# Values laid out and summed like keys on 128 partitions, their sums transposed on TensorE, and the first pass planned anew

## The chip, the cores and the metric

The kernel runs on one core of a Trainium2 chip. The metric is the device time of one execution in microseconds (us): the median of several executions. All times before come from three executions and from one more that was profiled.

## What is computed

Attention over pooled keys and values, and behind it two gated layers, all in 32-bit floats:

```python
B, H, S, D = 8, 8, 576, 64              # q, k, v
k_p = k.reshape(B, H, 72, 8, D).mean(axis=3)
v_p = v.reshape(B, H, 72, 8, D).mean(axis=3)
scores = D ** -0.5 * q @ k_p.T           # per head: 576 x 72
attn = softmax(scores)
x = (attn @ v_p) as 4608 tokens x 512
h = x @ w_in;  g = h * sigmoid(1.702 * h);  x = g @ w_out          # d_ff 2048
out = ((x @ w_a) * (x @ w_b)) @ w_o2                                # d_ff 1536
```

## The kernel before

The 4608 tokens are 9 blocks of 512 (called j), a block is 4 units of 128 tokens (called u, 36 of them), and a batch has 576 tokens, so 4.5 units. The layers run in passes over all blocks. The first pass also holds the whole attention, and makes the first 2 to 6 of the 16 feed-forward chunks (called f) of each block. The later passes are not touched.

The work of the first pass is a list of small tasks that `first_tasks` writes with what each waits for and which buffers it takes and gives back. The names are: `lk`, `lv` load half of a batch's keys or values (4 heads of 8); `skr`, `sv` sum 8 neighbours on VectorE (DVE); `ska` copies key sums into the block-diagonal tile `kbd` on ScalarE (ACT); `lq` loads a unit's queries; `sc` are the scores on TensorE (PE); `mx` the maxima (DVE), `ex` the exponentials (ACT), `b2` the division (DVE); `pt` the transposes of the attention weights (PE, tile `pt`) and `cp` their copy (ACT, tile `aT`); `px` the product with the value sums (PE); `hi` and `lo` split its result into two parts of a block's `x` (ACT, DVE); `xh`, `xl` store that; `lw` loads half of a weight chunk and `cva`, `cvb`, `cvh`, `cvl` turn it from 64-bit words into a two-part tile `w` (ACT, DVE); `h` are the 12 matmuls of the first product of a chunk, `th`, `st`, `gh`, `gl` its gate; `y` the second product into four `acc` tiles; `ev` and `ys` evict and store them through two `ys` buffers. A block's first `h` needs all four `lo` of its block.

`first_plan` places the tasks on the engines by the table COST and some lengths beside it (DELAY), with priorities shifted by LEAN, and the program then issues them in that order; every engine keeps it (`pin`). Where PE would idle before the first `y`, it gets matmuls on a tile `busy` whose result nobody reads. The DMAs all go through one queue, that of SP, in plan order; the built program lets a DMA there wait for the eighth one before it, among others. In the built program a `sc`, `px` or `busy` matmul of the listing is two in the trace, a transpose is one.

Before, the values of a batch lie with the 72 pooled positions on the partitions: a load is 72 rows, of 2048 numbers for batches 0 and 1 (half a batch, 576 KB) and of 1024 for the others (a quarter, 288 KB), and the sum is a reduction on 72 partitions, L474. The keys lie with two heads' 64 columns on 128 partitions: 128 rows of 1152 numbers, 576 KB, L447, summed at L453.

Of the kernel before, what the change touches and what calls it, by code (L numbers as in the profile page):

```python
# [10 lines left out]
F32 = mybir.dt.float32  # L11
# [3 lines left out]
ALU = mybir.AluOpType  # L15
AX = mybir.AxisListType
# [8 lines left out]
UNIT = 128  # L25

COST = dict(
    k=1.51, q=.67, v=1.51, vq=.76, w=1.34, x=2.69, p=.67,
    skr=1.28, ska=.68, sc=.49, mx=.40, ex=1.19, b2=1.12, pt=.44, cp=.50, px=.48, hi=.51, lo=.61, sv=2.21, svq=1.14,
    cva=.58, cvb=1.53, cvh=.54, cvl=2.40, h=2.72, th=.51, st=.61, gh=.54, gl=.61, y=.682, eva=.51, evd=.61,  # L30
)
DELAY = dict(PE=.24, ACT=.12, DVE=.12, SP=2.2)
TURN = .1
ROOM = dict(ps=4, acc=3, at=2, aT=3, tmp=2, g=1, gg=2, ks=2, kraw=1, vraw=2, q=2, xs=3, raw=2, yp=2, w=19)
LEAN = dict(
    svq=-12, cvl=-6, skr=-14, v=-5, k=3, mx=29, cp=37, vq=8, cvb=-4, cvh=-20, h=-1, q=3, pt=26, gl=13, sv=4,
    ex=6, th=41, gh=-4, w=-10, ska=7, cva=6, sc=1, eva=-1,
)
SPARE_UNITS = 6
LOOSE_UNITS = 14  # L40
FILL = 2.5
ACT_EVICTS = 3

# [1 line left out]
def first_tasks(counts, seq, chunks_made, per):  # L45
# [11 lines left out]
    for b in range(nb * per * UNIT // seq):  # L57
        scored, used = [], []
        if b >= 2:
            last = ((b - 1) * seq - 1) // UNIT  # L60
            scored = [f"sc{last}.{e}" for e in range(2)]
            used = [f"px{last}.{e}" for e in range(2)]
        for e in range(2):
            home = ["w"] if b < 2 else ["kraw"]
            add(f"lk{b}.{e}", "SP", "k", takes=home)
            add(f"skr{b}.{e}", "DVE", "skr", [f"lk{b}.{e}"], ["ks"], home)
            add(f"ska{b}.{e}", "ACT", "ska", [f"skr{b}.{e}"] + scored, (), ["ks"])
        for e in range(2 if b < 2 else 4):
            home = ["w"] if b < 2 else ["vraw"]
            add(f"lv{b}.{e}", "SP", "v" if b < 2 else "vq", takes=home)  # L70
            add(f"sv{b}.{e}", "DVE", "sv" if b < 2 else "svq", [f"lv{b}.{e}"] + used, (), home)
    for u in range(nb * per):
        j = u // per
        bank = "any" if u < SPARE_UNITS else "ps"
# [11 lines left out]
        for e in range(2):  # L86
            back = ([f"px{u - 1}.0"] if e else [f"px{u - 2}.1"]) if u >= per else [f"px{u - 2}.{e}"] if u >= 2 else []
            add(
                f"pt{u}.{e}", "PE", "pt", [f"b2{u}"] + back + ([f"pt{u}.0"] if e else []), [bank],
                ([] if u == 2 else ["w"] if u == 3 else ["at"]) if e else [],  # L90
            )
            add(f"cp{u}.{e}", "ACT", "cp", [f"pt{u}.{e}"], ["aT"], [bank])
            need = [n for b in batches(u) for n in ([f"sv{b}.{e}"] if b < 2 else [f"sv{b}.{2 * e}", f"sv{b}.{2 * e + 1}"])]
# [55 lines left out]
def first_plan(tasks):  # L149
# [41 lines left out]
    while len(start) < len(tasks):  # L191
# [16 lines left out]
        for p in members.get(n, [n]):  # L208
            kind = tasks[p][1]
            for r in tasks[p][3]:  # L210
                if r == "any":
                    r = bank[holder(p)] = "acc" if room["acc"] > 0 else "ps"
                room[r] -= 1
            start[p] = s
            s += COST[kind]
            if engine == "PE":
                s += 0. if (kind in ("h", "y")) == large else TURN
                large = kind in ("h", "y")
            free[engine] = s
            end = s + DELAY[engine]  # L220
            for r in tasks[p][4]:
                heapq.heappush(gives, (end, bank[holder(p)] if r == "any" else r))
            for m in after[p]:
                left[m] -= 1
                ready[m] = max(ready.get(m, 0.), s if tasks[m][0] == engine else end)
                if not left[m]:
                    queue[tasks[m][0]].append(m)
    return start, bank
# [3 lines left out]
def tile_kernel(ctx, tc, q, k, v, w_in, w_out, w_a, w_b, w_o2, out):  # L232
# [13 lines left out]
    nc = tc.nc  # L246
    P = 128
    NU, _, NP, _ = q.shape
    B, SP, H, D, _ = v.shape
    NT, DM = out.shape  # L250
    S = SP * POOL
    DFF, DFF2 = w_out.shape[0], w_o2.shape[0]
# [161 lines left out]
        nc.gpsimd.memset(t, 0.0)  # L414

    q_t, ks_t, vs_t, at_t, aT_t, kraw_t, vraw_t = {}, {}, {}, {}, {}, {}, {}
    sc_t, pt_t, px_t, x_full = {}, {}, {}, {}

    def pieces(u):
# [6 lines left out]
            done += n  # L426

    scale = 1.0 / (POOL * D ** 0.5)
    V = 2
    early = {}  # L430

    def load_q(u):
# [8 lines left out]
    def load_k(b, half):  # L441

        if b < 2:
            raw = wp.tile([P, 2, S], F32, tag="w", name="kvraw")
        else:
            raw = ap_.tile([P, 2, S], F32, tag="kraw", name="kraw", bufs=1)
        pin("SP", nc.sync.dma_start(out=raw, in_=k[b, :, 2 * half:2 * half + 2, :]))  # L447
        kraw_t[b, half] = raw

    def sum_k(b, half):  # L450
        ks = ks_t[b, half] = ap_.tile([P, 2, SP], F32, tag="ks", name="ks", bufs=2)
        raw = kraw_t.pop((b, half)).rearrange("p c (s r) -> p c s r", r=POOL)
# [8 lines left out]
    def load_v(b, n):  # L461
        heads = H // 2 if b < 2 else V
        if b < 2:
            raw = wp.tile([SP, heads, D, POOL], F32, tag="w", name="kvraw")
        else:
            raw = ap_.tile([SP, heads, D, POOL], F32, tag="vraw", name="vraw", bufs=2)
        pin("SP", nc.sync.dma_start(out=raw, in_=v[b, :, n * heads:(n + 1) * heads]))
        vraw_t[b, n] = raw

    def sum_v(b, n):  # L470
        if b not in vs_t:
            vs_t[b] = ap_.tile([SP, H, D], F32, tag="vs", name="vs", bufs=2)
        heads = H // 2 if b < 2 else V
        pin("DVE", nc.vector.tensor_reduce(  # L474
            out=vs_t[b][:, n * heads:(n + 1) * heads, :], in_=vraw_t.pop((b, n)), op=ALU.add, axis=AX.X
        ))
# [755 lines left out]
```

## Time and profile before

| | us |
|---|---|
| three executions | 1782.6, 1787.7, 1789.05 |
| median | 1787.7 |
| the profiled execution, its own time | 1786.03 |
| its span, from the first to the last instruction | 1784.2 |
| PE busy / DVE busy / ACT busy in the span | 1749.2 / 1033.8 / 610.6 |

The span is the part that the trace shows; 1.8 us of the execution's time lie around it. A busy PE is one that has a matmul in its pipeline; the records overlap, and at a lower granted clock a matmul counts for longer, so busy time is not useful time.

### The profile page before, as it was taken

How to read it: one execution, taken by the hardware profiler on the slowest of the kernel's cores; microseconds unless marked ns; L12 is line 12 of the kernel's file. 1: busy time of each engine (PE TensorE's matmuls, PEld its weight loads, DVE VectorE, ACT ScalarE, POOL GpSimd, SP SyncE). 2: the span in 40 equal slices, each digit the busy share in tenths (PEclk: the TensorE clock that was granted, in tenths of full speed). 3: DMA queues.
4: the chain of work that ended last, by engine and by line, in shares of the span. 5: the costliest groups of instructions: out<-in, count | busy, mean ns of one | idle time of the engine just before them, and what ended most of it. 6: DMA issues, size and time to landing. Idle time of an engine off the chain costs nothing.

```text
span 1784.2 us, 22457 instructions
## 1 busy us (share of the span) xinstructions
PE 1749.2 (98%) x8610; PEld 1449.4 (81%) x8610; DVE 1033.8 (58%) x1769; ACT 610.6 (34%) x1495; POOL 1.7 (0%) x8
## 2 busy tenths in 40 slices
PE   7989999999999999999999999999999999999999
PEld 6778788888888888888887788878788888788887
DVE  6888996448526668677756655733444444434443
ACT  5767675433223323334333322222121211221121
POOL 0000000000000000000000000000000000000000
PEclk8999999999999999999999999999999999999999
DMA  7656652434312565636596785678545659536612
GB/s 241 212 195 227 211 181 93 177 118 130 112 53 118 183 216 224 230 155 254 204 361 248 289 303 178 227 272 333 203 136 182 242 208 333 227 129 238 236 56 89
DMA packets 86987, 357.99 MB, mean 201 GB/s; under 512 B 9728, under 2 KB 9728, under 8 KB 61888
## 3 DMA queue, kind: packets, MB, share of 16 engines
q1 hardware_dynamic: 86880, 356.55, 55.2%
q8 instruction: 68, 1.11, 0.3%
q14 instruction: 39, 0.32, 0.1%
HBM read 238.55 MB, written 117.96 MB: 200 GB/s over the span
## 4 chain that ended last, share of the span: by engine, by line
PE 87%; DVE 6%; DMA 5%; ACT 1%; issue 0%; SPq 0%; DVEq 0%; ACTq 0%
PE X L737 16%; PE Y L737 8%; PE acc L332 7%; PE acc L333 7%; PE acc L334 7%; PE h L332 7%; PE h L334 6%; PE h L333 6%; PE acc L692 5%; PE acc L690 5%; PE acc L691 5%; PE Z L737 4%; DMA part<-ys 2%; PE px L543 1%; PE pt L528 1%; PE sc L496 1%
## 5 line engine op out<-in xcount | busy, mean ns | idle before, releaser
L737 PE MATMUL X<-xo,wc 128*128 128x512 f32 (+1 forms) x1440 | 330.4, 370 | 5.2 <-DVE s L755 4.4
L737 PEld LDWEIGHTS X<-xo,wc 128*128 128x128 f32 x1440 | 255.5, 189 | 58.8 <-DVE s L755 11.7
L332 PE MATMUL h<-x,w 128*128 128x512 f32 x576 | 226.3, 393 | 1.3 <-DVE x L558 0.7
L333 PE MATMUL acc<-glo,w 128*128 128x512 f32 x576 | 225.5, 391 | 0.0
L334 PE MATMUL acc<-ghi,w 128*128 128x512 f32 x576 | 225.2, 391 | 0.0
L333 PE MATMUL h<-x,w 128*128 128x512 f32 x576 | 224.3, 389 | 0.4 <-DVE x L558 0.4
L334 PE MATMUL h<-x,w 128*128 128x512 f32 x576 | 224.3, 389 | 0.0
L332 PE MATMUL acc<-ghi,w 128*128 128x512 f32 x576 | 190.6, 397 | 3.2 <-ACT ys L1132 3.2
L737 PE MATMUL Y<-xo,wc 128*128 128x512 f32 (+1 forms) x720 | 167.5, 368 | 0.0
L660 DVE SCALAR_TENSOR_TENSOR g<-g,h 128x512 f32<-128x512 f32 x100 | 68.6, 686 | 154.3 <-ACT g L657 154.2
L722 ACT CAST ghi<-s 128x512 fp32r<-128x512 f32 (+1 forms) x60 | 34.7, 578 | 335.5 <-DVE s L756 335.5
L737 PEld LDWEIGHTS Y<-xo,wc 128*128 128x128 f32 x720 | 128.4, 189 | 23.7
L657 ACT ACTIVATE g<-h 128x512 f32<-128x512 f32 x100 | 59.8, 598 | 228.2 <-PE h L334 194.9
L751 DVE TENSOR_TENSOR s<-s,Y 128x512 f32<-128x512 f32 (+1 forms) x60 | 38.1, 634 | 170.5 <-PE Y L737 170.2
L332 PEld LDWEIGHTS acc<-ghi,w 128*128 128x128 f32 x576 | 108.6, 189 | 28.0 <-ACT ys L1132 3.7
L332 PEld LDWEIGHTS h<-x,w 128*128 128x128 f32 x576 | 108.1, 188 | 25.6 <-ACT aT L534 1.6
L334 PEld LDWEIGHTS acc<-ghi,w 128*128 128x128 f32 x576 | 108.8, 189 | 23.1
L333 PEld LDWEIGHTS h<-x,w 128*128 128x128 f32 x576 | 108.2, 188 | 22.5 <-DVE x L558 0.7
L334 PEld LDWEIGHTS h<-x,w 128*128 128x128 f32 x576 | 108.1, 188 | 22.6
L333 PEld LDWEIGHTS acc<-glo,w 128*128 128x128 f32 x576 | 108.7, 189 | 21.4
L798 DVE TENSOR_TENSOR part<-acc,part 128x512 f32<-128x512 f32 x72 | 49.7, 692 | 78.8 <-PE acc L692 78.5
L661 ACT CAST ghi<-g 128x512 fp32r<-128x512 f32 x100 | 62.2, 622 | 92.7 <-DVE g L660 64.2
(102 smaller groups left out, 2651.1 us busy)
## 6 DMA issues: line engine op xcount, KB each, us to landing
xo<-yd SPq DMA_DIRECT2D x84, 1024.0 KB
yd<-st SPq DMA_DIRECT2D x28, 1024.0 KB
part<-part SPq DMA_DIRECT2D x108, 256.0 KB
xd<-x SPq DMA_DIRECT2D x18, 1024.0 KB
part<-ys SPq DMA_DIRECT2D x72, 256.0 KB
x<-xd SPq DMA_DIRECT2D x18, 1024.0 KB
raw<-in_moe_w_out_dram SPq DMA_DIRECT2D x28, 512.0 KB
wd<-ws SPq DMA_DIRECT2D x12, 1024.0 KB
```

The source lines that it names most:

```text
L332: nc.tensor.matmul(out=o, lhsT=whi, rhs=xhi, start=first, stop=False),
L333: nc.tensor.matmul(out=o, lhsT=whi, rhs=xlo, start=False, stop=False),
L334: nc.tensor.matmul(out=o, lhsT=wlo, rhs=xhi, start=False, stop=last),
L657: nc.scalar.activation(out=g, in_=hps, func=AF.Tanh, scale=0.5 * 1.702)
L660: made = (nc.vector.scalar_tensor_tensor(out=g, in0=g, scalar=1.0, in1=hps, op0=ALU.add, op1=ALU.mult))
L661: nc.scalar.copy(out=ghi, in_=g)
L690: after_last(nc.tensor.matmul(out=oa, lhsT=chi[:, ts], rhs=whi, start=first, stop=False))
L691: after_last(nc.tensor.matmul(out=oa, lhsT=chi[:, ts], rhs=wlo, start=False, stop=False))
L692: after_last(nc.tensor.matmul(out=oa, lhsT=clo[:, ts], rhs=whi, start=False, stop=last))
L737: after_last(nc.tensor.matmul(out=banks[nm], lhsT=w[:, at_, we, ks], rhs=x[:, xe, kk, :], start=n in FIRST and kk == 0 and m == 0, stop=kk ...
L751: nc.vector.tensor_tensor(out=s[2], in0=s[2], in1=Y, op=ALU.add)
L798: nc.vector.tensor_tensor(out=t, in0=a, in1=t, op=ALU.add)
```

## The change

Three things change together.

- The values get the keys' layout, 128 partitions and 1152 numbers a load for every batch, and the same functions load (`load_kv`) and sum them (`sum_kv`). The sums then stand the wrong way round for `px`, so four transposes a batch on PE (`vt`) turn them into one PSUM bank, and one ACT copy (`vc`) puts that into the tile `vs`, which `px` reads as before.
- From batch 2 on, keys and values share one ring of two raw tiles instead of one for the keys and two for quarter values; the sums share a ring of four.
- The table of the planner is new: other lengths for loads and stores (weights 1.65 for 1.34, `x` 3.2 for 2.69), an extra lateness for stores, other room, and other priorities. So the whole order of the first pass is another one. What each block computes, and how many chunks it takes in the first pass, stays.

```diff
 COST = dict(
-    k=1.51, q=.67, v=1.51, vq=.76, w=1.34, x=2.69, p=.67,
-    skr=1.28, ... px=.48, hi=.51, lo=.61, sv=2.21, svq=1.14,
+    k=1.45, q=.67, v=1.45, w=1.65, x=3.2, p=.67,
+    skr=1.28, ... px=.48, hi=.51, lo=.61, sv=1.28, vt=.44, vc=.50,
 )
-DELAY = dict(PE=.24, ACT=.12, DVE=.12, SP=2.2)
+DELAY = dict(PE=.24, ACT=.12, DVE=.12, SP=2.3)
+LATE = dict(x=4., p=1.)
-ROOM = dict(..., aT=3, ..., ks=2, kraw=1, vraw=2, ...)
+ROOM = dict(..., aT=4, ..., ks=4, raws=2, vs=2, ...)
-LOOSE_UNITS = 14
+LOOSE_UNITS = 16
...
+        home, bank = (["w"], "any") if b < 2 else (["raws"], "ps")
         for e in range(2):
+            for load, total in (("lk", "skr"), ("lv", "sv")):
+                add(f"{load}{b}.{e}", "SP", load[1], takes=home)
+                add(f"{total}{b}.{e}", "DVE", total, [f"{load}{b}.{e}"], ["ks"], home)
             add(f"ska{b}.{e}", "ACT", "ska", [f"skr{b}.{e}"] + scored, (), ["ks"])
-        for e in range(2 if b < 2 else 4):
-            home = ["w"] if b < 2 else ["vraw"]
-            add(f"lv{b}.{e}", "SP", "v" if b < 2 else "vq", takes=home)
-            add(f"sv{b}.{e}", "DVE", "sv" if b < 2 else "svq", [f"lv{b}.{e}"] + used, (), home)
+        add(f"vt{b}", "PE", "vt", [f"sv{b}.{e}" for e in range(2)], [bank], ["ks", "ks"])
+        add(f"vc{b}", "ACT", "vc", [f"vt{b}"] + used, (), [bank])
...
-            need = [... f"sv{b}.{e}" ...]
+            need = [f"vc{b}" for b in batches(u)]
...
-                ready[m] = max(ready.get(m, 0.), s if tasks[m][0] == engine else end)
+                ready[m] = max(ready.get(m, 0.), s if tasks[m][0] == engine else end + LATE.get(tasks[m][1], 0.))
...
+    def turn_v(b):
+        vt = vt_t[b] = bank_of(f"vt{b}", [SP, NP, P])
+        for c in range(NP):
+            after_last(nc.tensor.transpose(vt[:, c, :], vsum_t[b, c // 2][:, c % 2, :], ident))
+
+    def copy_v(b):
+        vs_t[b] = ap_.tile([SP, H, D], F32, tag="vs", name="vs", bufs=2)
+        pin("ACT", nc.scalar.copy(out=vs_t[b].rearrange("s h d -> s (h d)"), in_=vt_t.pop(b).rearrange("s c n -> s (c n)")))
...
-        if name == "v":
-            return a.reshape(b, h, s // POOL, POOL, d).transpose(0, 2, 1, 4, 3)
         a = a.reshape(b, h // 2, 2, s, d).transpose(2, 4, 1, 0, 3)
-        if name == "k":
+        if name != "q":
             return a.transpose(3, 0, 1, 2, 4).reshape(b, 2 * d, h // 2, s)
```

The order moves everywhere in the first pass; two places are shown. First SP's queue near the start of the program, from the fourth query load on, before (`kvraw` and `vraw` are raw keys or values, `qs` and `q` queries, `raw` a weight half):

```order
L439 DMA qs<-in_q_dram 128x512
L439 DMA q<-in_q_dram 128x512 x2
L447 DMA kraw<-in_k_dram 128x1152
L467 DMA kvraw<-in_v_dram 72x2048
L467 DMA vraw<-in_v_dram 72x1024 x2
L467 DMA kvraw<-in_v_dram 72x2048 x2
L439 DMA q<-in_q_dram 128x512
L447 DMA kraw<-in_k_dram 128x1152
L439 DMA q<-in_q_dram 128x512
L467 DMA kvraw<-in_v_dram 72x2048
L640 DMA raw<-in_moe_w_in_dram 128x1024
L640 DMA raw<-in_moe_w_out_dram 128x1024
```

and the same place with the change, again from the fourth query load on:

```order
L441 DMA qs<-in_q_dram 128x512
L449 DMA kvraw<-in_v_dram 128x1152 x2
L449 DMA kvraw<-in_k_dram 128x1152
L634 DMA raw<-in_moe_w_in_dram 128x1024
L441 DMA q<-in_q_dram 128x512
L634 DMA raw<-in_moe_w_out_dram 128x1024
L441 DMA q<-in_q_dram 128x512
L449 DMA kvraw<-in_v_dram 128x1152 x2
L634 DMA raw<-in_moe_w_in_dram 128x1024
L449 DMA kvraw<-in_k_dram 128x1152 x2
L634 DMA raw<-in_moe_w_out_dram 128x1024
L441 DMA q<-in_q_dram 128x512 x2
```

The first weight halves moved from behind all values of batches 0 and 1, and behind values and keys of batch 2, to right behind batch 0's values; the values of batch 2 are no longer among the first loads.

Second, PE's order from the first product with values on (`px`; the scores of units 0 to 5 stand ahead of it). Before:

```order
L543 MATMUL px<-aT,vs 64x128 x8
L368 MATMUL busy<-ident 128x128 x6
L543 MATMUL px<-aT,vs 64x128 x8
L368 MATMUL busy<-ident 128x128 x11
L528 MATMUL pt<-ident,at_203 72x128 x16
L543 MATMUL px<-aT,vs 64x128 x8
L528 MATMUL pt<-ident,at 72x128 x4
L543 MATMUL px<-aT,vs 64x128 x4
L528 MATMUL pt<-ident,at 72x128 x4
L543 MATMUL px<-aT,vs 64x128 x4
L528 MATMUL pt<-ident,at 72x128 x4
L496 MATMUL sc<-kbd_136,q 128x144 x4
```

Behind these stand `px` and `pt` of units 4 and 5, more scores and two `busy`, and then the first `h`. With the change, from the last transposes ahead of the first `vt` on (scores of units 0 to 3 stand ahead):

```order
L522 MATMUL pt<-ident,at 72x128 x16
L370 MATMUL busy<-ident 128x128 x7
L466 MATMUL vt<-ident,ks 72x128 x4
L370 MATMUL busy<-ident 128x128 x3
L537 MATMUL px<-aT,vs 64x128 x4
L522 MATMUL pt<-ident,at_184 72x128 x4
L537 MATMUL px<-aT,vs 64x128 x4
L522 MATMUL pt<-ident,at_184 72x128 x4
L537 MATMUL px<-aT,vs 64x128 x4
L522 MATMUL pt<-ident,at_184 72x128 x4
L537 MATMUL px<-aT,vs 64x128 x4
L522 MATMUL pt<-ident,at_184 72x128 x4
```

Behind these stand 16 `px`, the scores of unit 4 (16 matmuls in the trace) and of half of unit 5's count (8), the second `vt`, three `busy`, and the first `h`. So before, six units are through their `px` ahead of the first `h`; with the change four are, and the scores of two more.

## Rows read from the trace of the kernel before

**Rows 1.** Busy time by stretch (--windows): PE, PEld, DVE, ACT, POOL, granted clock, DMA share, GB/s.
```profile
0.00:54.84 54.84, 41.93 (x310) 35.60 (x311) 34.39 (x56) 32.90 (x145) 1.73 (x8) 0.81 0.69 220
54.84:210.00 155.16, 146.83 (x951) 119.12 (x950) 139.29 (x249) 112.66 (x413) 0.00 (x0) 0.98 0.67 227
210.00:380.00 170.00, 169.19 (x1027) 140.80 (x1026) 109.88 (x200) 92.97 (x308) 0.00 (x0) 1.00 0.41 144
```

**Rows 2.** What PE waited for from 0 to 500: us in total, times, longest.
```profile
PE px L543 <- DVE vs L474: 5.9, 3, 4.0
PE pt L528 <- DVE at L522: 4.6, 2, 4.2
PE acc L332 <- ACT ys L1132: 3.2, 1, 3.2
```

**Rows 3.** PE's timeline, the first matmul of a feed-forward chunk: start, length.
```profile
54.84 0.47 PE L332 MATMUL h<-x,w 128*128 128x512 f32 x1
```

**Rows 4.** DVE's timeline, sums that waited for a load.
```profile
4.68 2.76 DVE L453 TENSOR_REDUCE ks<-kvraw 128x144 f32<-128x1152 f32 x2 [4.68 <-DMA kvraw<-in_k_dram]
...
8.98 1.35 DVE L453 TENSOR_REDUCE ks<-kvraw 128x144 f32<-128x1152 f32 x1 [0.28 <-DMA kvraw<-in_k_dram]
...
34.45 2.28 DVE L474 TENSOR_REDUCE vs<-kvraw 72x256 f32<-72x2048 f32 x1 [4.05 <-DMA kvraw<-in_v_dram]
```

**Rows 5.** PE's groups before 55 us (--lines): busy, mean ns; idle before.
```profile
L528 PE MATMUL pt<-ident,at 128*72 128x128 f32 x48 | 9.6, 361 | 5.2 <-DVE at L522 4.2 <-DVE sm L520 0.9
L543 PE MATMUL px<-aT,vs 72*64 72x128 f32 x80 | 8.4, 369 | 4.5 <-DVE vs L474 4.5
L496 PE MATMUL sc<-kbd,qs 128*128 128x144 f32 x32 | 5.0, 300 | 0.9 <-DMA qs<-in_q_dram 0.9
L496 PE MATMUL sc<-kbd,q 128*128 128x144 f32 x24 | 4.5, 344 | 0.0
```

**Rows 6.** The chain that ended last, in order of time: start, length, what.
```profile
43.43 1.00 PE pt L528 x4
44.43 1.05 PE px L543 x8
...
48.53 1.83 PE sc L496 x8
55.65 2.43 ACT at L512 x16
...
69.85 0.70 DVE raw L628
...
132.65 0.49 PE sc L496 x4
133.14 0.87 PE pt L528 x8
...
137.25 1.02 PE px L543 x16
```

**Rows 7.** Busy time by stretch again, two stretches of the start.
```profile
20.00:30.00 10.00, 5.49 (x48) 4.83 (x49) 5.60 (x6) 6.44 (x40) 0.00 (x0) 0.81 1.04 275
...
40.00:50.00 10.00, 10.00 (x59) 7.52 (x58) 4.24 (x11) 5.04 (x9) 0.00 (x0) 0.50 0.12 48
```

**Rows 8.** ACT's timeline: the first exponentials.
```profile
8.15 0.32 ACT L512 ACTIVATE at<-sc,mx 128x72 f32<-128x72 f32 x1
```

**Rows 9.** Groups of DVE and ACT from 0 to 380.
```profile
L474 DVE TENSOR_REDUCE vs<-vraw 72x128 f32<-72x1024 f32 x24 | 28.7, 1207 | 1.7 <-DMA vraw<-in_v_dram 1.7
...
L453 DVE TENSOR_REDUCE ks<-kraw 128x144 f32<-128x1152 f32 x12 | 16.1, 1346 | 2.4 <-DMA kraw<-in_k_dram 2.4
...
L534 ACT COPY aT<-pt 72x512 f32<-72x512 f32 x72 | 39.3, 589 | 20.9 <-PE pt L528 19.5 <-PE px L543 1.3
```

**Rows 10.** PE's transposes from 55 to 210 (--lines).
```profile
L528 PE MATMUL pt<-ident,at 128*72 128x128 f32 x136 | 18.5, 274 | 1.1 <-ACT aT L534 0.4 <-DVE at L522 0.4 <-ACT at L512 0.3
```

More of the change, by code (lines that the diff above doesn't have):

```diff
@@ L27 @@
 COST = dict(
-    k=1.51, q=.67, v=1.51, vq=.76, w=1.34, x=2.69, p=.67,
-    skr=1.28, ska=.68, sc=.49, mx=.40, ex=1.19, b2=1.12, pt=.44, cp=.50, px=.48, hi=.51, lo=.61, sv=2.21, svq=1.14,
+    k=1.45, q=.67, v=1.45, w=1.65, x=3.2, p=.67,
+    skr=1.28, ska=.68, sc=.49, mx=.40, ex=1.19, b2=1.12, pt=.44, cp=.50, px=.48, hi=.51, lo=.61, sv=1.28, vt=.44, vc=.50,
     cva=.58, cvb=1.53, cvh=.54, cvl=2.40, h=2.72, th=.51, st=.61, gh=.54, gl=.61, y=.682, eva=.51, evd=.61,
 )
-DELAY = dict(PE=.24, ACT=.12, DVE=.12, SP=2.2)
+DELAY = dict(PE=.24, ACT=.12, DVE=.12, SP=2.3)
+LATE = dict(x=4., p=1.)
 TURN = .1
-ROOM = dict(ps=4, acc=3, at=2, aT=3, tmp=2, g=1, gg=2, ks=2, kraw=1, vraw=2, q=2, xs=3, raw=2, yp=2, w=19)
+ROOM = dict(ps=4, acc=3, at=2, aT=4, tmp=2, g=1, gg=2, ks=4, raws=2, vs=2, q=2, xs=3, raw=2, yp=2, w=19)
 LEAN = dict(
-    svq=-12, cvl=-6, skr=-14, v=-5, k=3, mx=29, cp=37, vq=8, cvb=-4, cvh=-20, h=-1, q=3, pt=26, gl=13, sv=4,
-    ex=6, th=41, gh=-4, w=-10, ska=7, cva=6, sc=1, eva=-1,
+    mx=83, gl=42, lo=90, st=59, b2=57, px=21, pt=77, sv=2, vt=-3, gh=-19, ska=-29, cvh=-7, th=14, vc=5,
+    eva=-5, cp=-1, p=-8, evd=4, x=5,
 )
 SPARE_UNITS = 6
-LOOSE_UNITS = 14
+LOOSE_UNITS = 16
 FILL = 2.5
@@ L92, in first_tasks @@
             add(f"cp{u}.{e}", "ACT", "cp", [f"pt{u}.{e}"], ["aT"], [bank])
-            need = [n for b in batches(u) for n in ([f"sv{b}.{e}"] if b < 2 else [f"sv{b}.{2 * e}", f"sv{b}.{2 * e + 1}"])]
+            need = [f"vc{b}" for b in batches(u)]
             add(f"px{u}.{e}", "PE", "px", [f"cp{u}.{e}"] + need + ([f"px{u}.0"] if e else []), [] if e else [bank], ["aT"])
@@ L135, in holder @@
         return "pt" + name[2:]
+    if kind in ("vt", "vc"):
+        return "vt" + name[2:]
     return "px" + name[2:].split(".")[0]
@@ L248, in tile_kernel @@
     NU, _, NP, _ = q.shape
-    B, SP, H, D, _ = v.shape
+    B, SP, H, D = k.shape[0], k.shape[3] // POOL, 2 * NP, q.shape[1] // 2
     NT, DM = out.shape
@@ L416, in tile_kernel @@
     q_t, ks_t, vs_t, at_t, aT_t, kraw_t, vraw_t = {}, {}, {}, {}, {}, {}, {}
+    vsum_t, vt_t = {}, {}
     sc_t, pt_t, px_t, x_full = {}, {}, {}, {}
@@ L428, in tile_kernel @@
     scale = 1.0 / (POOL * D ** 0.5)
-    V = 2
     early = {}
@@ L439, in load_q, with load_kv @@
         pin("SP", nc.sync.dma_start(out=q_t[u], in_=q[u]))
-    def load_k(b, half):
+    def load_kv(src, raws, b, half):
         if b < 2:
@@ L445, in load_k, with sum_kv @@
         else:
[L446 to L452, printed above, removed]
+            raw = ap_.tile([P, 2, S], F32, tag="kvraw", name="kvraw", bufs=ROOM["raws"])
+        pin("SP", nc.sync.dma_start(out=raw, in_=src[b, :, 2 * half:2 * half + 2, :]))
+        raws[b, half] = raw
+    def sum_kv(raws, totals, b, half):
+        ks = totals[b, half] = ap_.tile([P, 2, SP], F32, tag="ks", name="ks", bufs=ROOM["ks"])
+        raw = raws.pop((b, half)).rearrange("p c (s r) -> p c s r", r=POOL)
         pin("DVE", nc.vector.tensor_reduce(out=ks, in_=raw, op=ALU.add, axis=AX.X))
@@ L459, in to_kbd @@
         pin("ACT", nc.scalar.mul(out=kbd[b % 2][D:P, cs, SP:2 * SP], in_=ks[D:P], mul=scale))
[L461 to L476, printed above, removed]
+    def turn_v(b):
[5 more added lines that the diff above has]
+        pin("ACT", nc.scalar.copy(out=vs_t[b].rearrange("s h d -> s (h d)"), in_=vt_t.pop(b).rearrange("s c n -> s (c n)")))
     def bank_of(name, shape):
@@ L1139, in tile_kernel @@
     does = dict(
-        lk=load_k, skr=sum_k, ska=to_kbd, lv=load_v, sv=sum_v, lq=load_q, sc=scores, mx=maxima, ex=exps, b2=normalise,
+        lk=lambda b, e: load_kv(k, kraw_t, b, e), skr=lambda b, e: sum_kv(kraw_t, ks_t, b, e), ska=to_kbd,
+        lv=lambda b, e: load_kv(v, vraw_t, b, e), sv=lambda b, e: sum_kv(vraw_t, vsum_t, b, e), vt=turn_v, vc=copy_v,
+        lq=load_q, sc=scores, mx=maxima, ex=exps, b2=normalise,
         pt=transposes, cp=copy_aT, px=averages, hi=lambda u: x_part(u, 0), lo=lambda u: x_part(u, 1),
```

3 lines of the change are left out of this document (removed).

## The prediction

> **What bounds the kernel now.** I read the busy time by stretch first, cut at the first feed-forward matmul and at 210 us [rows 1]. From 210 on PE is never short of work (169.19 of 170 us at the full clock), and the later passes, which the change leaves alone, are of that kind too. So the end moves by whatever useless PE time goes away before 210 us, and by whatever PE work is added. The reader should see two lossy stretches. In the first, up to 54.84 us, PE is busy for only 41.93 us, at a granted clock of 0.81 in the mean. In the second, 54.84 to 210, it idles for 155.16 - 146.83 = 8.3 us, and a clock of 0.98 costs 0.02 x 155 = 3.1 us more.
>
> How much of the first stretch was useful? The first `h` starts at 54.84 [rows 3]. Ahead of it PE did 56 score matmuls, 48 transposes and 80 `px` matmuls of full size [rows 5], and by the listing 16 scores of half height and 32 `px` of half width. Packed, as the chain shows them at full clock, four scores take 0.49 us, eight transposes 0.87, sixteen `px` 1.02 [rows 6]: 0.1225, 0.109 and 0.064 each. That is 6.9 + 5.2 + 5.1, and 2.0 for the half-size ones at half price: 19.2 us. So **35.6 of the first 54.84 us are lost, and 11.4 of the next 155**.
>
> The waits say why. Value sums kept `px` waiting for 5.9 us in three waits, and the divided weights `at` kept `pt` waiting for 4.6 [rows 2]; the second is the first again, since the divisions of units 2 to 5 stand behind the four value sums in DVE's order, and the last of these got its values at 34.45 [rows 4]. Then comes the clock: between 40 and 50 us PE is busy without a gap, but with `pt` and `px` alternating and at 0.50, the lower level [rows 7]; four transposes take 1.00 us there, eight `px` 1.05 and eight scores 1.83 [rows 6].
>
> **The change, part by part.** *Loads.* With keys and queries in flight, four transfers (two key halves of 128 x 1152 numbers, 0.59 MB, and two query units of 128 x 512, 0.26 MB: 1.70 MB) land between 4.68 and 8.98 [rows 4], 395 GB/s. With the 72-row values in flight it is 275 GB/s, with the 16 DMA engines busy throughout (1.04) [rows 7]. In the new queue the second half of batch 1's values is the sixteenth transfer. Ahead of and with it go 4 key halves and 4 value halves of 0.59 MB, 6 query units of 0.26 and two weight halves of 0.52, 7.34 MB. From the 2.29 MB at 8.98 on, that is 12.8 us at 395 GB/s or 18.4 at 275: landed at 21.8, or 27.3, against 34.45. The first weight half (5.11 MB in) lands at 16.1 or 19.2. The lower bound would hold if the new layout changed nothing in the rate; I take the upper, since the new rows have the form of the keys'.
>
> *The chain on ACT and DVE to the first `h`.* ACT starts on exponentials at 8.15 [rows 8]; keys and order are unchanged up to there. Eight half units follow at 2.43 us for two [rows 6]: 17.9. Behind them on ACT, up to the cast of the first weight half, stand two weight copies, eight `cp`, `vc`, a pair of `kbd` and two `hi`. With the 0.59 us of a `cp` for each of the 14 (a `kbd` pair counted as one, its pieces being smaller) and for the cast, 15 x 0.59 = 8.9 [rows 9]: 26.8. DVE then needs the four last steps of the weight half, at most 0.70 us each [rows 6], and two `lo` of the same size: 4.2, so 31. The value sums of batch 1 fit in ahead of it: this chain is late next, not the loads.
>
> *PE's chain.* `vt` of batch 0 can't start before the last sums on DVE, some 1 us behind the exponentials, so `px` starts near 20.5, when ACT has made three `cp` and `vc`. Up to `h` stand 8 pieces of 8 `px`, 4 pieces of 4 `pt`, 16 half and 8 full scores, `vt`, six `busy`. At the lower level: 8 x 1.05 + 4 x 1.00 + 3.7 (scores, at 0.23 and 0.115 each) + 1.0 + 1.4 (a `busy` taken as a score) = 18.5, so 39. At the upper about half: 30, and then the 31 of ACT and DVE decides. Before, the stretch of alternating `pt` and `px` ran at the lower level; the new order has such a stretch too, between scores. It comes here after only short gaps, not after 4 us of idling, so I take the middle, **first `h` at 35** (31 to 39).
>
> By then the new order has done 40 full and 16 half scores, 32 transposes and 64 `px`: 4.9 + 1.0 + 3.5 + 4.1 = 13.5 us of useful work. So 35 - 13.5 = 21.5 us are lost instead of 35.6: **14.1 gained** (10 to 18).
>
> *The second stretch.* DVE is its tightest engine: 139.29 of 155.16 us busy [rows 1]. The sums of a batch from batch 2 on were four of 1207 ns and become two of 1346 [rows 9]: 2.1 us less for each of six batches, 12.8 us in all. In return DVE starts the stretch some 20 us earlier with less done ahead. The largest single wait there, 3.2 us of `acc` behind an eviction [rows 2], comes from the two `ys` buffers; the new order puts scores, a `vt`, an `h`, `px` and `pt` between the blocks in question, before it was one `h`. The 11.4 lost us can't all go, as every wait shifts; none of them need go, if a new wait takes each one's place. **I take 6** (0 to 11.4), half, since DVE has 12.8 us less to do but PE's order is as tight as before.
>
> *What is added.* Four transposes a batch. The two batches ahead of the first `h` are in the chain above. Of the six others, 24 transposes at 0.109 us [rows 6], **2.6 us** go on PE; with 0.25 (the lower level) 6.0. The ACT copies, six of 0.59 us, are covered: ACT has 42 us free in the second stretch [rows 1]. Without that cover they would cost 3.5.
>
> The Trainium skill (TensorE: Matmul & The Clock Gate, Part 4: PE-mode transpose) gives about 275 ns for a transpose in a kernel, which speaks against the change: 24 of them would cost 6.6 us instead of 2.6, and the sum below would end near 1772.5. This trace has a record of 274 ns, as the page says [rows 10], but eight of them pass in 0.87 us, so the records overlap and the page's figure is not what one adds here.
>
> **Sum.** 14.1 + 6 - 2.6 = 17.5 us. The profiled execution took 1786.03 (its span 1784.2, and 1.8 around it): **1768.5**. The median of the three shown is 1787.7, 1.7 above the profiled one, so this may read as much as 1770; I leave it at 1768.5. With the bounds: 10 + 0 - 6 gives 1782, 18 + 11.4 - 2.6 gives 1759.
>
> **Rivals.** *All goes well (1753 to 1761).* PE keeps the upper level at the start, the first `h` comes at 31, and the second stretch loses almost nothing. For it: the new start has no gap like the 4 us before 34.45. Against: the low clock between 40 and 50 us with PE busy [rows 7]. 18 + 10 - 2.6: 1760.
>
> *The start's gain is handed back (1776 to 1784).* An earlier start brings DVE's work on weights, 11 chunks of it, closer together; PE then waits for `glo` or `w` instead of for values. The second stretch loses 6 us more than before instead of 6 less: 14.1 - 6 - 2.6 = 5.5, 1780.5. For it: DVE already 90% busy. Against: the 12.8 us taken off it. It is also what remains if the loads gain nothing and PE is slow: the first `h` at 39 and no gain behind it, 10 - 2.6: 1778.6.
>
> *Slower than before (over 1786).* Keys and values of batches 2 to 7 now share two raw tiles, and SP's queue is served in order. A load that waits for a tile holds up queries, weights and stores behind it; the halves needed by `vt` come last. If each of six batches kept PE waiting, the gain is gone from 17.5 / 6 = 2.9 us a batch on. The nearest rows are the wait for a first value (4.05 us [rows 4]) and for an eviction (3.2): at 4.05 a batch, 24.3, the time is 1793. For it: fewer buffers in flight than the three before. Against: a tile is free again after a sum of 1.35 us [rows 9].
>
> **How the numbers follow.** Likeliest, 1768.5, with its own range 1761 to 1776: 0.60. All well: 0.14. Handed back: 0.19. Slower: 0.07. The range of 1757 to 1782 leaves out the slower case, a third of the good one and the last part of the handed-back one, some 0.17. What can be told from no change is 0.5%, 8.9 us: below 1778.8 is faster, above 1796.6 slower. Faster: 0.60 + 0.14 and 0.08 of the handed-back case, 0.82. Same: the other 0.11 and 0.03 of the slower case: 0.14. Slower: 0.04.
>
> **What the profile would show.** Right: first `h` between 31 and 39, the last of batch 1's values summed before 29, DVE waiting for values nowhere near 4 us; PE idle in the second stretch (to 190) below 6 us; `vt` records of some 270 ns but 0.44 us for four; the stretch from 380 on as long as now. The step on PE's clock is wrong if the start shows 1.00 throughout, or 0.50 from 13 us to the first `h`. The sum is wrong if PE's new waits name `vs`, `glo` or `w` for more than 8 us, or if a store that is not done keeps ACT and then PE waiting more than once.

## The result, and the profile after

The changed kernel takes **1761.76 us** (median of 4 runs, 1760.76 to 1762.62); the kernel before took 1788.24 beside it (4 runs, 1782.6 to 1789.05). The ratio is 0.9858, 95% interval [0.9837, 0.988]: faster, by 6.7 us more than the 17.5 of the forecast sum against the execution that was profiled (1786.03), and inside the range. The profiled execution took 1762.6, its span 1760.8 against 1784.2: 23.4 us to explain. Some of them belong to the execution that was profiled before: its mean granted clock is 0.990, and in the groups of runs below, where the kernel before has 0.990 to 0.996, its median is 1782.6 to 1783.0. The changed kernel's medians lie 18.6 and 21.7 us under that there.

Busy time by stretch of the changed kernel, cut at its first `h`, at 187 us (23 ahead of the 210 of [rows 1]) and 170 us later (columns as there: PE, PEld, DVE, ACT, POOL, granted clock, DMA share, GB/s):

```profile
0.00:29.92 29.92, 24.95 (x218) 21.72 (x219) 23.82 (x39) 22.59 (x91) 1.74 (x8) 1.00 0.86 329
29.92:187.00 157.08, 153.65 (x1052) 125.40 (x1051) 150.16 (x279) 128.45 (x479) 0.00 (x0) 1.00 0.74 253
187.00:357.00 170.00, 170.00 (x1038) 141.75 (x1038) 96.28 (x177) 91.67 (x305) 0.00 (x0) 1.00 0.38 132
357.00:1760.80 1403.80, 1388.84 (x6318) 1151.97 (x6316) 749.72 (x1265) 370.92 (x630) 0.00 (x0) 1.00 0.55 204
```

The first row ends 25 us earlier than in [rows 1], and its granted clock is 1.00 where it was 0.81. The second loses 157.08 - 153.65 = 3.4 us where it lost 11.4, at 1.00 for 0.98. The last row, 1403.80, is the 1404.2 that were left of the span before from 380 on: the gain is all in the first 187 us.

What PE waited for in the changed kernel, 0 to 400 us (in total, times, longest), against [rows 2]:

```profile
PE pt L522 <- DVE at L516: 1.9, 2, 1.0
PE acc L334 <- ACT ys L1126: 1.1, 1, 1.1
PE vt L466 <- DVE ks L455: 0.7, 1, 0.7
...
PE px L537 <- ACT vs L470: 0.7, 1, 0.7
```

The waits for values (5.9 before) have shrunk to two of 0.7, that of `vt` for the sums and that of `px` for `vs`; those for `at` from 4.6 to 1.9. Why, DVE's timeline shows: the two sums of batch 1's values, and the last `lo` ahead of the first `h`, with no wait for a load in any of them:

```profile
22.33 1.35 DVE L455 TENSOR_REDUCE ks<-kvraw 128x144 f32<-128x1152 f32 x1
...
24.57 1.34 DVE L455 TENSOR_REDUCE ks<-kvraw 128x144 f32<-128x1152 f32 x1
...
28.82 1.28 DVE L552 TENSOR_TENSOR x<-px,x 128x512 fp32r<-128x512 f32 x2
```

In [rows 4] the last of those sums started at 34.45, having waited 4.05. The transfers behind it, in the row of 10 to 20 us:

```profile
10.00:20.00 10.00, 7.93 (x64) 6.83 (x62) 9.73 (x20) 10.00 (x58) 0.00 (x0) 1.00 1.03 410
```

With the DMA engines as full as in [rows 7] (1.03 against 1.04), they move 410 GB/s and not 275.

### The profile page after: what moved, and what is told of

It reads as the page before. It is cut to its first block, busy times and chain, and to the rows that moved or that the text cites. A ratio compares the mean times of both kernels' runs of the same rounds, so it can differ in the third digit from the quotient of the medians.

```text
span 1760.8 us, 22461 instructions
## 1 busy us (share of the span) xinstructions
PE 1737.5 (99%) x8620; PEld 1440.8 (82%) x8620; DVE 1020.0 (58%) x1757; ACT 613.6 (35%) x1503; POOL 1.7 (0%) x8
## 4 chain that ended last, share of the span: by engine, by line
PE 93%; DVE 3%; DMA 2%; ACT 1%; issue 0%; SPq 0%; DVEq 0%; ACTq 0%
PE X L731 17%; PE Y L731 8%; PE acc L334 7%; PE acc L336 7%; PE h L334 7%; PE acc L335 7%; PE h L336 7%; PE h L335 7%; PE acc L686 5%; PE acc L684 5%; PE acc L685 5%; PE Z L731 4%; DMA part<-ys 2%; PE px L537 2%; PE sc L490 1%; PE pt L522 1%
## 5 line engine op out<-in xcount | busy, mean ns | idle before, releaser
L334 PEld LDWEIGHTS h<-x,w 128*128 128x128 f32 x576 | 108.1, 188 | 23.3 <-issue 1.4
L336 PEld LDWEIGHTS acc<-ghi,w 128*128 128x128 f32 x576 | 108.1, 188 | 23.3 <-DVE w L626 0.4
```

What stands on the lines that cost most here:

```text
L334: nc.tensor.matmul(out=o, lhsT=whi, rhs=xhi, start=first, stop=False),
L336: nc.tensor.matmul(out=o, lhsT=wlo, rhs=xhi, start=False, stop=last),
```

## The experiments

The questions were: what the start's gain is made of (loads, order, clock), whether it is DVE's lighter load that emptied the second stretch, what a `vt` costs, and what the kernel could still gain. Over the runs, theory 1 is that the start is gained by value loads at the full rate, in an order that uses them, and by a clock that then stays up; each expectation says what that makes of its run. The runs came in three groups, each with runs of the kernel before on the same chip: without the fillings, the two halves and the transposes twice beside 1782.61 (10 runs); the changed kernel again, more fillings in the kernel before, 72 rows and four tiles beside 1782.88 (17 runs); the others beside 1783.01 (12 runs).

**The changed kernel again** (no edit).

> The changed kernel once more, beside the others of this group on one chip: 1760 to 1763 by every theory, first h at 29 to 31 and the granted clock at 1.00 up to there.

1764.24 (6 runs, 1759.67 to 1768.25), ratio 0.9894 [0.9874, 0.9913]: the expectation missed. In the profiled execution the clock fell at the start, which it had not done in the first profile. Its row of 20 to 30 us (the columns of all such rows are those of [rows 1]):

```profile
20.00:30.00 10.00, 8.95 (x62) 5.88 (x63) 7.49 (x11) 6.67 (x14) 0.00 (x0) 0.60 0.60 240
```

PE's timeline has the first `h`:

```profile
37.13 0.48 PE L334 MATMUL h<-x,w 128*128 128x512 f32 x1
```

So the same program has its first `h` at 29.92 or at 37.13, by whether PE keeps the upper level (2.4 GHz) or goes to the lower (1.2), here from 22.1 to 35.7 us. The span is 1764.4, only 3.6 more: 1.8 comes back at a late wait (below), which is 3.1 here instead of 4.9, and the clock is low for 3.4 us behind it instead of 6.8, which is another 1.7.

> The changed kernel once more, beside the others of this call: 1760 to 1766; first h at 30 where the clock stays up through the start, 36 to 37 where it falls.

1761.35 (5 runs, 1758.57 to 1767.2), ratio 0.9889 [0.9872, 0.9906]; in this profile the clock stayed up and the first `h` came at 29.90.

The mean granted clock of every execution is known, and it tells the two kinds apart. Of the changed kernel's 15 (four of the result, 6 and 5 here), ten have 0.998 to 1.000 and took 1758.57 to 1763.22; four have 0.994 or 0.995 and took 1765.86 to 1768.25; one lies between (0.997, 1765.27). The first kind's mean is 1761.2, the second's 1766.9, so an estimate from these is that the fall costs 5.7 us. All four executions of the result are of the first kind.

**Without the fillings** behind the first group:

```diff
-                keep_busy(int((start[name] - pe_free) * FILL))
+                if not busy:
+                    keep_busy(int((start[name] - pe_free) * FILL))
```

> The changed kernel without its filling matmuls, but for the first ten; the rest of the order is the same. Theory 1: the clock stayed at 2.4 GHz in the new start because the two fills between the scores of unit 3 and the first px keep PE at work; without them the granted clock falls to 0.50 before 25 us, pt, px and scores up to the first h take up to twice their time, the first h comes at 35 to 39 instead of 29.9, and the time is 1767 to 1771. Theory 2: the new order has no gap long enough for a fall, fills or not: the first h stays at 29 to 30.5 and the time at 1760 to 1763.

1769.2 (4 runs, 1767.51 to 1770.35), ratio 0.9929 [0.9915, 0.9944], against 0.9858, 0.9889 and 0.9894 of the three groups of runs of the changed kernel. Its row of 20 to 30 us:

```profile
20.00:30.00 10.00, 9.34 (x59) 6.27 (x61) 7.29 (x10) 6.05 (x13) 0.00 (x0) 0.50 0.60 241
```

The clock is at the lower level from 19.6 to 36.7 and once more at 43.5 to 50.3, and the first `h` starts at 36.93, 7 us late. All four executions have a mean granted clock of 0.991 or 0.992: theory 1 holds as to the clock in the changed kernel.

**The halves of the change.** First the new layout with the old table (COST, DELAY, LEAN, LOOSE_UNITS as before, no LATE):

```diff
-    k=1.45, q=.67, v=1.45, w=1.65, x=3.2, p=.67,
+    k=1.51, q=.67, v=1.51, w=1.34, x=2.69, p=.67,
-LATE = dict(x=4., p=1.)
+LATE = dict()
...
-LOOSE_UNITS = 16
+LOOSE_UNITS = 14
```

> The new layout of the values with the planner's old table (old lengths, priorities, no lateness; the room that the new tasks need). Theory 1: each part gives about half. The values of batch 1 then land near 24 us instead of 34.5, the sums are shorter, but six units still stand ahead of the first h and the weights come last: first h near 45, and DVE has the 12.8 us less to do: 1774 to 1779. Theory 2: the order is what counts, the layout gives nothing by itself: 1784 to 1789. Theory 3: the layout is nearly everything: 1762 to 1767.

1774.85 (4 runs, 1772.82 to 1775.96), ratio 0.9961 [0.9946, 0.9975]. Then the old layout with the new table, the kernel before with the opposite edit:

> The old layout of the values (72 rows, sums of 2.28 and 1.21 us, no transposes) planned with the new table. Theory 1: each part gives about half: the weights come early, four units ahead of the first h by the plan, but the slow value loads and long sums hold it until 40 to 45, and the second stretch loses as much as before: 1773 to 1780. Theory 2: order alone: 1761 to 1767. Theory 3: layout alone: 1784 to 1790.

1777.46 (7 runs, 1774.28 to 1779.11), ratio 0.9966 [0.9953, 0.9979]. The row of 10 to 20 us of each; first new layout and old table:

```profile
10.00:20.00 10.00, 8.70 (x74) 7.62 (x75) 9.86 (x19) 9.94 (x55) 0.00 (x0) 1.00 0.99 388
```

and old layout with the new table:

```profile
10.00:20.00 10.00, 6.87 (x54) 6.05 (x54) 9.34 (x19) 8.43 (x57) 0.00 (x0) 1.00 1.01 284
```

The layout sets the rate (388 against 284 GB/s with the DMA engines equally full), the table sets what is asked for first. Alone they bring the first `h` to 52.07 and 49.70, 3 and 5 us forward, together 25; in time, 7.8 and 5.2 us of the medians, together about 20. That the two need each other is shown by this; what holds each up is shown in part. With the new layout alone PE still does six units ahead of the first `h`, with the new table alone the old rows load slowly, and in both the clock falls as well (0.50 from 30 to 40 us with the new layout, 0.57 from 20 to 40 with the new table). Both times lie in what theory 1 expected, but both first `h` came later than its 45, and 40 to 45.

The second stretch tells the halves apart. Its rows, from the first `h` of each on; first new layout and old table, then old layout and new table:

```profile
52.07:207.00 154.93, 150.36 (x1020) 124.30 (x1019) 149.29 (x270) 121.64 (x432) 0.00 (x0) 1.00 0.71 246
```

```profile
49.70:205.00 155.30, 148.98 (x977) 122.29 (x977) 148.83 (x267) 118.11 (x427) 0.00 (x0) 0.99 0.69 232
```

With the new layout alone 4.6 us are lost there, with the new table alone 6.3 and 1.6 for the clock, where it was 11.4 before and 3.4 with both. So the layout brings most of it (6.8), the table some (3.5).

**The rate alone**: the changed kernel, with the values of batches 0 and 1 loaded as 72 rows of 2048 numbers, as before, in the new places of the queue. Sums are then made on 72 partitions, of 1152 numbers each, so the output isn't that of the reference.

```diff
+        if b < 2 and raws is vraw_t:
+            raw = wp.tile([P, 2048], F32, tag="w", name="kvraw")
...
+            pin("SP", nc.sync.dma_start(out=raw[0:SP], in_=rows_[at_:at_ + SP]))
...
+            pin("DVE", nc.vector.tensor_reduce(out=ks[0:SP], in_=raw, op=ALU.add, axis=AX.X))
```

> The changed kernel with the value loads of batches 0 and 1 back on 72 rows of 2048 numbers (as many bytes, same place in the queue); their sums take 1152 numbers of 72 rows, so their result is not the values' sums, at the same length of 1.35 us on DVE. Theory 1: the layout's gain at the start is the transfer rate: batch 1's values then land 4 to 6 us later than now, DVE waits for them, and the first h comes at 33 to 36: 3 to 6 us more. Theory 2: the place in the queue is what counts, since values land some us before DVE takes them: first h within 1 us of 29.9 and the time within 1.5 us.

1770.59 (6 runs, 1765 to 1771.92), ratio 0.9931 [0.9913, 0.9949], 6.3 us over the changed kernel of the same group. Rows of 10 to 30 us:

```profile
10.00:20.00 10.00, 8.85 (x68) 8.42 (x67) 8.73 (x19) 9.35 (x62) 0.00 (x0) 1.00 1.00 296
20.00:30.00 10.00, 8.17 (x96) 6.02 (x95) 6.94 (x11) 9.20 (x21) 0.44 (x2) 1.00 0.90 248
```

The same bytes as 72 rows go at 296 GB/s and less, and the first `h` starts at 34.84, 4.9 us later than the 29.92, at a clock of 1.00 in both. DVE's timeline has the sums of batch 1's values, which now wait for their loads:

```profile
26.50 1.35 DVE L464 TENSOR_REDUCE ks<-kvraw 72x144 f32<-72x1152 f32 x1 [1.61 <-DMA kvraw<-in_v_dram]
...
29.75 1.35 DVE L464 TENSOR_REDUCE ks<-kvraw 72x144 f32<-72x1152 f32 x1 [1.31 <-DMA kvraw<-in_v_dram]
```

They started at 22.33 and 24.57, without a wait, in the changed kernel. That is the rate by itself. The medians' 6.3 is not all of that kind: the profiled execution, the fastest (1765.0), has a mean granted clock of 0.998, the five others (1768.97 to 1771.92) have 0.993 or 0.994, so that the clock falls more often here.

**The clock alone, in the kernel before.** More fillings in its two waits for values, 48 of them (96 in the trace, which has two records for each):

```diff
-                keep_busy(int((start[name] - pe_free) * FILL))
+                more = {"px1.0": 20, "pt2.0": 28}.get(name, 0)
+                keep_busy(int((start[name] - pe_free) * FILL) + more)
```

> The kernel before with 48 more filling matmuls (96 in the trace) in the two places where PE waited for value sums, between 23 and 38 us; nothing else is changed. Theory 1: part of what the kernel before lost at its start is the clock and not the late values: the values still land at 34.5, but the transposes and px from 38 to 50 us then run at 2.4 GHz and the first h comes at 47 to 50 instead of 54.8, so the time falls by 5 to 8 us. Theory 2: the clock falls all the same in the stretch of transposes and px, or what is won is waited away behind it: within 2 us of the kernel before.

1790.15 (10 runs, 1785.03 to 1792.86), ratio 1.0033 [1.0019, 1.0047]: slower by more than either theory had. In the profiled execution the clock stayed at 1.00 until 45.2. That is the fastest of the ten (1785.03) and the only one with a mean granted clock of 0.997, where the others have 0.993 or 0.994; it too is no faster than the median of the kernel before. PE's timeline, with a wait in it, and the first `h`:

```profile
38.47 1.74 PE L528 MATMUL pt<-ident,at 128*72 128x128 f32 x12 [1.09 <-DVE at L522]
43.93 0.63 PE L528 MATMUL pt<-ident,at 128*72 128x128 f32 x4 [3.72 <-DVE x L558]
...
57.00 0.48 PE L332 MATMUL h<-x,w 128*128 128x512 f32 x1
```

DVE's timeline of the same time:

```profile
35.02 2.28 DVE L474 TENSOR_REDUCE vs<-kvraw 72x256 f32<-72x2048 f32 x1 [4.56 <-DMA kvraw<-in_v_dram]
...
43.19 1.28 DVE L558 TENSOR_TENSOR x<-px,x 128x512 fp32r<-128x512 f32 x2
```

PE, now at full speed, ran into DVE. DVE starts its last value sum at 35.02, when the load has come, and then works without a gap through four units' divisions and a weight half to the `lo` at 43.19. The fourth group of transposes waited for the bank that this `lo` frees; in the kernel before, it ran right behind the third, ahead of the `lo` at 42.62, so it had another bank. With fewer fillings the transposes were to keep the old one, so they were tried:

```diff
+                more = {"px1.0": 14, "pt2.0": 20}.get(name, 0)
```

> The kernel before with 34 filling matmuls in its two waits for values (20 to 24 and 33 to 37 us), few enough that the fourth group of transposes at 40 us keeps its accumulator bank (in the run with 48 fillings it got another bank and waited 3.7 us for VectorE) (result unchanged). Theory: the clock stays up to 43 us or more, and with the wait for the bank gone the first h comes at 52 to 53.5 instead of 54.84; that is all the clock is worth without the faster values: 1 to 2.5 us faster, ratio 0.9985 to 0.9995. Rival 1, that the fall of the clock alone set the late start: first h at 45 or earlier, 8 us or more faster. Rival 2, that fillings in themselves hold up the start: first h at 57 again.

1789.4 (5 runs, 1786.88 to 1790.45), ratio 1.0037 [1.0025, 1.0049]: the theory's 1 to 2.5 us did not come; rival 2 was the nearest. PE's timeline:

```profile
43.09 1.09 PE L543 MATMUL px<-aT,vs 72*64 72x128 f32 x16 [2.15 <-DVE x L558]
...
55.59 0.48 PE L332 MATMUL h<-x,w 128*128 128x512 f32 x1
```

and its row of 40 to 50 us:

```profile
40.00:50.00 10.00, 7.85 (x56) 5.79 (x55) 3.79 (x8) 4.42 (x8) 0.00 (x0) 0.67 0.09 39
```

The transposes no longer wait for the `lo`, but the `px` behind them do (2.15 us), the clock falls there all the same, and the first `h` is at 55.59. The kernel before has no such wait; its `px` at the same place run ahead of the `lo` at 42.62:

```profile
41.46 1.98 PE L543 MATMUL px<-aT,vs 72*64 72x128 f32 x16
```

So both filled kernels have a wait for that `lo` which the kernel before does not have, and neither shows what the clock is worth by itself, nor that the bank is not the price. That the slow transposes of the kernel before fill a time in which DVE is not ready anyway (its `lo` ends at 43.90 there, at 44.47 and 43.63 in the filled ones) fits the missing gain, but is not shown to be its cause. Why both are 6 to 7 us slower than the kernel before by the median of their groups is open too: the first `h` is only 2.2 and 0.75 us later than in [rows 3], but that execution was 3 us over those medians.

**Transposes twice**: each `vt` made two times, 32 transposes more.

```diff
-        for c in range(NP):
+        for c in [c for c in range(NP) for _ in range(2)]:
```

> The changed kernel with each of the 32 transposes of value sums issued twice, 32 more. Theory 1: one adds its spacing in a packed row, 0.109 us, and the eight ahead of the first h are partly hidden: 2.6 to 3.5 us more than 1761.8, so 1764 to 1765.5. Theory 2: one adds its record of 0.272 us: 8.7 more, 1770.5. Theory 3: PE has room for them: below 1763.

1762.1 (4 runs, 1761.5 to 1763.59), ratio 0.9889 [0.9873, 0.9906]; span 1761.8, 1.0 more than the changed kernel's. One `vt` of the changed kernel and what follows it, and the same place with twice the number:

```profile
190.00 0.60 PE L466 MATMUL vt<-ident,ks 128*72 128x128 f32 x4
190.35 0.48 PE L334 MATMUL h<-x,w 128*128 128x512 f32 x1
```

```profile
191.59 1.03 PE L466 MATMUL vt<-ident,ks 128*72 128x128 f32 x8
192.38 0.47 PE L334 MATMUL h<-x,w 128*128 128x512 f32 x1
```

From start to start, four pass in 0.35 us and eight in 0.79, so each one added takes 0.11; a record of one is some 272 ns long, as they overlap. Where the last `vt` start, with 28 more ahead of them, PE stands 2.5 us later than in the changed kernel (298.28 against 295.81), and behind them, with all 32, 2.9 (299.07 against 296.17): 0.09 each. At the late wait 1.9 of it come back (3.0 for 4.9). So the time alone fits theory 3 (below 1763), but PE had no room for them: theory 1's price is paid in the first pass, and most of it comes back at the late wait.

**VectorE's relief taken back**: the value sums of batches 2 to 7 made twice.

```diff
-        pin("DVE", nc.vector.tensor_reduce(out=ks, in_=raw, op=ALU.add, axis=AX.X))
+        for _ in range(2 if raws is vraw_t and b >= 2 else 1):
+            pin("DVE", nc.vector.tensor_reduce(out=ks, in_=raw, op=ALU.add, axis=AX.X))
```

> The changed kernel with the value sums of batches 2 to 7 done twice on VectorE (12 sums more at 1.346 us, 16.2 us of VectorE, all behind the start; result unchanged). Theory: what the second stretch regained (lost time 11.4 before, 3.4 after) came from VectorE's lighter load, so handing it 16.2 us back costs about what was regained: 4 to 8 us over the changed kernel of the same call, and more waiting of TensorE on VectorE between first h and 187 us (lost 8 or more of that stretch). Rival: VectorE had slack there (150.2 of 157.1 us busy, but TensorE is the bound) and the gain came from the transfers and the order alone: under 2 us.

1774.48 (7 runs, 1772.6 to 1780.99), ratio 0.9958 [0.9944, 0.9973], 13.1 over the changed kernel of the same group. The clock fell at the start in the profiled execution (first `h` 36.77), so the 157.2 us from 36.8 on are compared with the same stretch of the changed kernel in the profile with the fall (first `h` 37.13); first with the sums twice:

```profile
36.80:194.00 157.20, 147.73 (x1000) 119.39 (x1001) 149.38 (x264) 121.62 (x455) 0.00 (x0) 0.98 0.70 236
```

and the changed kernel:

```profile
36.80:194.00 157.20, 154.17 (x1056) 125.94 (x1055) 148.91 (x274) 128.73 (x479) 0.00 (x0) 1.00 0.73 253
```

Of PE's waits from 0 to 400 with the sums twice, two that the changed kernel doesn't have:

```profile
PE h L334 <- DVE g L1094: 2.7, 1, 2.7
...
PE h L334 <- DVE x L553: 2.1, 2, 1.6
```

In this stretch PE idles 9.5 us instead of 3.0, above all for `g` and `x` from DVE, and the clock's 0.02 of 157 adds 3. DVE is busy for 149 us in either; the extra work only goes further behind. The theory holds, and at more than its 4 to 8. The start's clock is not what makes the 13.1: the spans of these two profiles, both with the fall, are 1778.0 and 1764.4, 13.6 apart.

**Evictions to four tiles.** In the changed kernel the largest wait behind the first pass is in the third, where results go out through two `ys` tiles. PE's wait from 1100 to 1300:

```profile
PE acc L684 <- ACT ys L796: 4.9, 1, 4.9
```

and the same wait in the kernel before:

```profile
PE acc L690 <- ACT ys L802: 3.6, 1, 3.6
```

The store ahead of that eviction is slow (issued at 1154.6, done about 1170, with the DMA engines moving 422 GB/s from 1160 on), and behind the wait the clock is at 0.5 for 6.8 us. Two of each four evictions were given tiles of their own:

```diff
-            t = yp.tile([P, N], F32, tag="y", name="ys")
+            t = yp.tile([P, N], F32, tag="y", name="ys") if c < 2 else p2.tile([P, N], F32, tag="part", name="part", bufs=4)
```

> The changed kernel with two of the four evictions of a block in the third pass group going to idle tiles of the later partial sums instead of all through the two ys tiles. Theory 1: PE's wait of 4.9 us near 1166 us, and the 6.8 us at half clock that follow it, come from these two tiles, whose stores land up to 16 us after their issue: both go, 5 to 8 us less than the changed kernel. Theory 2: the next wait is then for the loads that fill the DMA engines there (422 GB/s from 1160 to 1170), and less than 2 us are won.

1760.92 (5 runs, 1754.47 to 1762.75), ratio 0.9871 [0.985, 0.9892], 3.3 under the changed kernel of the same group, with overlapping intervals and less than the 5 to 8 of theory 1. In the trace the wait and the fall of the clock behind it are gone, and the span is 1759.1 against 1764.4; both of these executions had the fall at the start, the first `h` being at 36.34 and 37.13, so 0.8 of these 5.3 us are won at the start. One of the five executions has a mean granted clock of 1.000, and took 1754.47; the others have 0.995 or 0.996.

**The same with more fillings** in the three gaps of the start:

```diff
-                keep_busy(int((start[name] - pe_free) * FILL))
+                keep_busy(int((start[name] - pe_free) * FILL) + {"pt0.0": 7, "vt0": 7, "px0.0": 6}.get(name, 0))
```

> The changed kernel with two of the four evictions of each group of the third pass to tiles of their own (as in the four-out run) and 20 more filling matmuls, in the three gaps of TensorE at 13, 18 and 20 us (result unchanged). Theory: the clock's fall in some executions follows these gaps; with them filled, the clock is 1.00 up to the first h, which is at 30 to 31 us, and the four-out run's 1760.9 comes down by up to 3 to 4: 1755 to 1759, and the repeats spread less. Rival: the fillings hold up the real work by as much as they save, or the fall comes anyway: 1760 to 1763, first h at 36 or later.

**1755.34** (4 runs, 1754.91 to 1755.61), ratio 0.9847 [0.9835, 0.986], against [0.9872, 0.9906] of the changed kernel of the same group: the fastest of all, 6.0 us under that, and its runs lie within 0.7 us of each other, where the changed kernel's spread over 8.6. Its rows of the start:

```profile
10.00:20.00 10.00, 10.00 (x89) 9.88 (x88) 9.72 (x20) 10.00 (x59) 0.00 (x0) 1.00 1.03 411
20.00:30.00 10.00, 10.00 (x118) 8.23 (x118) 8.11 (x12) 7.61 (x16) 0.00 (x0) 1.00 0.60 240
```

PE has no gap left between 10 and 30 us. The first `h`, at 31.28, is 1.4 us later than in an execution of the changed kernel without the fall, and 5.9 earlier than in one with it. All four executions have a mean granted clock of 1.000, so the fall came in none of them, where it came in four of five with four tiles alone. The one without it there took 1754.47: the fillings win by keeping the clock up, not by themselves. Four executions can't show that the fall never comes.

## Why the prediction was right, point by point

**The mechanism was right, but for the clock.** Both lossy stretches gave, and the last stretch stayed. Of the things that the profile was to show, the sums of batch 1 are done at 25.91 (before 29 was asked), DVE waits for a key or value load only once, for the first (4.6 us), and the second stretch idles 3.4 us (below 6). Two signs of being wrong came. The start shows a clock of 1.00 throughout, which was to tell that the step on PE's clock is wrong. And a store that is not done stops ACT and then PE twice: for 1.1 us in the first pass, where ACT's eviction has waited for its `ys` tile, and for 4.9 in the third.

```profile
145.76 0.60 ACT L1126 ACTIVATE ys<-acc 128x512 f32<-128x512 f32 x1 [0.87 <-DMA part<-ys]
```

The kernel before has both waits too (3.2 and 3.6), so the sum does not fall with this sign; only the growth of the second is missing from it.

**The first `h`: the mis-sized term.** Forecast at 35, measured at 29.92, below the 31 to 39 that was given. Two of the three steps in it were right. *Loads*: I took 395 GB/s for the new rows, and it was 410; with the old rows in the new places the runs give 296. *ACT's and DVE's chain*: forecast to end at 31, and its last `lo` ended at 28.82 + 1.28 = 30.1, the `h` having started on what was ready at 29.92. *PE's chain* was the step that failed: I took the middle of 30 (upper level) and 39 (lower). The kernel does not run at a middle: an execution keeps the upper level and has its `h` at 29.9, or drops to the lower and has it between 36.3 and 37.1 (profiled executions of the changed kernel and of those with four tiles and with the sums twice). The forecast of 35 lies between the two and is neither. With 13.5 us of useful work, 29.92 - 13.5 = 16.4 are lost instead of 35.6: 19.2 gained for the 14.1 of the sum. With the fall it would be 12.0. The result shows the one kind because all four of its executions kept the clock up, which nothing in the forecast decided; with the fall they would have taken some 1766 to 1768, close to the forecast. So it is luck which side of the middle came, but either side lies in the range.

**The second stretch: 8.0 for 6.** The reason given, DVE's 12.8 us less, is shown by the run with the sums twice: with 16.2 us handed back, PE idles 6.5 us more there, and with the old table and the new layout only 4.6 us are lost. That the order has a part in it is shown too: with the old layout and the new table 7.9 are lost instead of 11.4. The forecast gave its reason for DVE alone.

**Transposes: 2.6.** By the doubled run 32 cost 2.9 in PE's position behind them, 0.09 each, 0.11 by the spacing of one group; 24 are 2.2 to 2.6. The overlap of records was read rightly.

**Not foreseen: 1.3.** The late wait for a store grew from 3.6 to 4.9. 19.2 + 8.0 - 2.6 - 1.3 = 23.3, and the span fell by 23.4.

**The rivals.** What came is close to *all goes well*, which had 1760 with the clock up, an `h` at 31 and a second stretch that loses almost nothing; it had a chance of 0.14 and deserved more. What spoke against it, the lower clock at 40 to 50 us before [rows 7], came there behind waits of 4 us that the change removes; with these waits filled, the clock of the kernel before stayed at 1.00 until 45.2 in one profile. It was not without weight either, as the changed kernel's clock falls in some executions behind gaps of at most 1.05 us. *The gain handed back* through DVE did not happen, but the doubled sums show how near it is: 16 us more on DVE bring most of it. *Slower*, through the shared raw tiles, has nothing for it: behind the start DVE waits for no key or value load, and the longest single wait of PE in the first pass is 1.1 us.

## What to carry to other kernels

A transfer's price is set by its layout as well as its bytes: compare GB/s at the same DMA share (275 and 410 here) before planning an order, and then plan the order anew, since layout and order each brought a quarter to two fifths of the gain alone. Where PE has short gaps ahead of its first long stretch, an execution can go either way on the clock, so look at the granted clock of every execution and not only of the profiled one. Fillings kept it up in four executions of four in the changed kernel; in the kernel before, where PE ran into VectorE, they won nothing, and moved a wait for a bank onto PE. What an engine wins early can be lost at a later wait for something that moves at its own pace, here a store, so look for the next such wait before counting the gain.

## What was not expected of the hardware

- One program keeps the clock at 1.00 through its start in some executions and has 0.5 from 22 to 36 us in others. It moves the first `h` by 7.2 us, the span of the two profiles by 3.6, and the mean time of the two kinds of execution by 5.7.
- With the DMA engines moving 422 GB/s, a store of 256 KB took about 16 us from issue to landing; two more tiles made the wait for it go away.
- Twenty fillings, which compute nothing that is used, brought the kernel with four tiles from 1760.92 to 1755.34 and its runs from within 8.3 us of each other to within 0.7 (in two groups of runs).
